# First two hidden units of the second token group in one-pass products, their operands split in the first group's last two units

## The chip, the cores and the metric

The kernel runs on one core of one Trainium2 chip. The metric is the device time of one execution in microseconds, as a median of several runs; less is better. The profile is one execution of its own.

## What is computed

An attention block without softmax, then a feed-forward block over all 4608 tokens:

```python
kv = einsum('bhsd,bhse->bhde', k, v)             # (8, 8, 64, 64)
o = einsum('bhsd,bhde->bhse', q, kv)             # (8, 8, 576, 64)
x = o / sqrt(mean(o * o, axis=-1) + 1e-6) * g_norm
x = x.transpose(0, 2, 1, 3).reshape(4608, 512)
h = x @ w_in                                     # w_in (512, 2048)
g = h * erf(softplus(h))
out = g @ w_out                                  # w_out (2048, 512)
```

q, k, v and g_norm are float32; w_in and w_out come as float64 and are turned into float32 on the chip.

## The kernel before

**Groups and units.** The 4608 tokens are worked off in nine groups of G = 512 (`NG`). Group T below 8 holds the first 512 tokens of batch T; group 8 holds the last 64 tokens of all eight. The 2048 columns of h are FC = 16 tiles of 128. One *unit* is one such tile of one group: h as a 128x512 block, which needs KC = 4 products of 128x128 by 128x512. The first FIRST = 2 groups are run by a loop over n = 0 to 32, with T, f = divmod(n, 16); seven more groups follow in batches of four units.

**Two kinds of product.** In the first group, a unit's h is a plain float32 product (L1031), one accumulation into one PSUM bank, copied out by `nc.scalar.copy`. A *one-pass* product (`hidden`, which calls `product`, L600) works on operands that are split: x into x_high, x_low and x_both, a weight tile into three parts as well. Twelve matmuls go into two banks: n_ps takes 8 (high and low), m_ps takes 4 (both). ACT copies n_ps with a scale, DVE adds m_ps (`add`, L575). The output product of a unit is plain in the first two groups: `project` (L656), four products into four banks that stay open over the units of a group. It runs LAG = 5 units behind h.

**How operands are split.** x: `upper` on ACT (L535), `lower_only` on DVE (L538), `both_only` on DVE (L541). A weight tile: `w_upper` on ACT (L559), `w_lower` with two DVE instructions (L562, L565) and a DMA on SP's queue that stores the parts to DRAM, from where all later groups load them. During the second group all 16 input tiles ("in") and all 16 output tiles ("out") are split, by a list `to_cut[f]` of tiles for each unit. A tile lives in one of four buffers of the pool `w_in_p` (then it is stored by one DMA), or at a place in memory that earlier weight tiles held (`w_place`, three DMAs). Units with f < WHOLE = 2 of the second group, n = 16 and 17, are still plain; from n = 18 on, h is one-pass, with the input tile that was split two units before. Input tiles 0 and 1 are split too, at n = 16 and 17, but only to be stored.

**Memory.** The pool `early` holds the raw weights and the first attention pairs. At n == FC = 16 it is closed, and `late`, `x_new`, `acc`, `w_in_p` and `low` are opened where it was. x of the second group, `xT[1]`, lies in the buffer "b" of the pool `wide`; x_high takes buffer "a", which held `xT[0]`, and x_both takes "b" once the last plain product of the second group has read `xT[1]`.

**Order.** The schedule is manual: each engine runs its instructions in the order in which the program emits them. For unit n: joins of raw weights while they are due (L271 to L282), `w_lower` for up to two weight tiles that `w_upper` took in the unit before, attention pieces, `gates` (L904, h times s of unit n - 4), the product of h, its copy, more splits, softplus (L1065), attention pieces, then `project(n - 5)`. Every fourth unit Erf is run for four units at once (L976), with an ACT table load before and after it. The pieces of attention for the second group's last pair lie around n = 12 to 15: `mean` with Ln, Exp and Square (L476 to L478) at n = 14, and `norm` on DVE (L484, L487, L496), which completes `xT[1]`, at n = 15, with the transpose of the next pair's q (L337). The first pair of the third group is visited at n = 17 (L412 to L426). At n = 16 x_high and x_low are made before h, at n = 17 x_both after it:

```python
if T == FIRST - 1:
    if f == 0:
        x_high = wide.tile([P, KC, G], FP32R, name="x_high", tag="a")
        x_low = low.tile([P, KC, G], FP32R, name="x_low")
        for i in range(0, KC, 2):
            upper(xT[T][:, i : i + 2], x_high[:, i : i + 2])
        for i in range(0, KC, 2):
            lower_only(xT[T][:, i : i + 2], x_high[:, i : i + 2], x_low[:, i : i + 2])
if T == FIRST - 1 and f >= WHOLE:
    n_ps, m_ps = hidden(T, f, turns=False)
```

Of the kernel before, what the change touches and what calls it, by code (L numbers as in the profile page):

```python
# [40 lines left out]
FP32R = mybir.dt.float32r  # L41
# [9 lines left out]
BATCH = 4  # L51
LAG = 5
# [1 line left out]


FIRST = 2
WHOLE = 2
SHIFT = 4096.0
SQ = 32
ORDER = """  # L60
# [9 lines left out]
def kernel(  # L70
# [11 lines left out]
    P = 128  # L82
# [3 lines left out]
    G = J * P  # L86
    R = S - G
    NP = H // 2
    KC = DM // P
    FC = DF // P  # L90
# [9 lines left out]
    wide = ctx.enter_context(tc.tile_pool(name="wide", bufs=1, side="right"))  # L100
# [189 lines left out]
    w_at = {"load": 0, "split": 0, "join": 0}  # L290
# [8 lines left out]
    def weights():  # L299

        w_next("split")
        w_next("join")
        w_next("load")
# [229 lines left out]
    def upper(x, high):  # L533

        nc.scalar.activation(high, x, AF.Copy, scale=1.0 + 2.0**-13)  # L535

    def lower_only(x, high, low):
        nc.vector.tensor_tensor(out=low, in0=x, in1=high.bitcast(FP32), op=ALU.subtract)  # L538

    def both_only(high, low, both):  # L540
        nc.vector.scalar_tensor_tensor(  # L541
            out=both,
            in0=low.bitcast(FP32),
            scalar=SHIFT,
            in1=high.bitcast(FP32),
            op0=ALU.mult,
            op1=ALU.add,
        )
# [80 lines left out]
    def w_lower(which, f):  # L629

        t, x, parts = w_new.pop((which, f))
        lower_w(x, *parts)
        kept = w_kept[which, f] = dram.tile([P, 3, G], FP32, name=f"w_{which}{f}")
        for i in range(3):
            if t is None:
                nc.sync.dma_start(out=kept[:, i], in_=parts[i].bitcast(FP32))
        if t is not None:
            nc.sync.dma_start(out=kept, in_=t.bitcast(FP32))
            if which == "in" and f >= WHOLE:
                w_now[which, f] = [t]  # L640

    def hidden(T, f, turns=True):
# [232 lines left out]

    others = [("in", f) for f in range(WHOLE)]
    others += [("out", f) for f in (*range(FC - BATCH, FC), *range(FC - BATCH))]
    places_w = {3: 0, 5: 1, 6: 0, 8: 1, 9: 2, 10: 0}  # L880
    held_w = {FC - 7: 3, FC - 5: 1}
    to_cut = {f: [] for f in range(FC)}
    for f in range(FC):
        if f < FC - BATCH:
            other = others.pop(0)
            if other[0] == "out" and other[1] in held_w:
                other = (*other, held_w[other[1]])
            to_cut[f] = [other, ("in", f + WHOLE)]
        elif f == FC - BATCH:
            to_cut[f] = [("in", FC - 2), ("in", FC - 1)]  # L890
        if f in places_w:
            to_cut[f].append((*others.pop(0), places_w[f]))
# [22 lines left out]
    def hold_lower(n):  # L915
        lower(hs[n], *g_held[n])
# [60 lines left out]

    for n in range(FIRST * FC + 1):
        T, f = divmod(n, FC)
        if n == FC:  # L980
            early_room.close()
            late = ctx.enter_context(tc.tile_pool(name="late", bufs=1))
            x_new = ctx.enter_context(tc.tile_pool(name="x_new", bufs=1))
            acc = ctx.enter_context(tc.tile_pool(name="acc", bufs=1))
            w_in_p = ctx.enter_context(tc.tile_pool(name="w_in_p", bufs=BATCH))
            low = low_room.enter_context(tc.tile_pool(name="low", bufs=1))
            forms = late.tile([P, 3, KC, G], FP32R, name="x_forms0")
            x_forms[FIRST] = [forms[:, i] for i in range(3)]
        if T < FIRST:
            if f == 0:  # L990
                steps = pieces_of(T + 1)

            if due(0 if n == 2 * (BATCH - 1) else 1):
                weights()
            while kept:
                keep_prepared()
            for piece in steps[f][3]:
                piece()
            for key in list(w_new)[:2]:
                w_lower(*key)  # L1000
            for piece in steps[f][0]:
                piece()
        while due(0):
            weights()
        done = n - LAG + 1
        if T == 0 and done >= 0:
            gates(done)
        if T == FIRST - 1:
            if f == 0:
                x_high = wide.tile([P, KC, G], FP32R, name="x_high", tag="a")  # L1010
                x_low = low.tile([P, KC, G], FP32R, name="x_low")
                for i in range(0, KC, 2):
                    upper(xT[T][:, i : i + 2], x_high[:, i : i + 2])
                for i in range(0, KC, 2):
                    lower_only(xT[T][:, i : i + 2], x_high[:, i : i + 2], x_low[:, i : i + 2])
        if T == FIRST - 1 and f >= WHOLE:
            n_ps, m_ps = hidden(T, f, turns=False)
        elif T < FIRST:

            if n >= AHEAD:  # L1020
                plain[n] = ps_h.tile([P, G], FP32, name="h_ps", tag="h")
                blocks = [(n, c) for c in range(KC)]
            elif n == 0:
                for i, (pool, tag) in enumerate(((ps_now[0], "at"), (ps_now[0], "at"), (ps_o, "o0"))):
                    plain[i] = pool.tile([P, G], FP32, name="h_ps", tag=tag)
                blocks = [(i, c) for c in range(2) for i in range(2)]
                blocks += [(2, 0), (2, 1)] + [(i, 2) for i in range(3)] + [(0, KC - 1)]
            else:
                blocks = [(n, KC - 1)]
            for i, c in blocks:  # L1030
                nc.tensor.matmul(  # L1031
                    plain[i],
                    lhsT=blocks_of(one(w_in_sb, i % FC))[:, c],
                    rhs=xT[T][:, c, :],
                    start=(c == 0),
                    stop=(c == KC - 1),
                )
        if T < FIRST:
            if n == whole:
                old_h = acc.tile([P, BATCH, G], FP32, name="h", tag="e")  # L1040
            h = hs[n] = old_h[:, n - whole] if n >= whole else unit("h_sb")
            s = ss[n] = unit("s_sb")
            if n in plain:
                nc.scalar.copy(h, plain.pop(n))
            else:
                nc.scalar.activation(h, n_ps, AF.Copy, scale=SHIFT - 1.0)
                add(h, m_ps)
            if T == FIRST - 1:
                if f == 1:
                    x_both = wide.tile([P, KC, G], FP32R, name="x_both", tag="b")  # L1050
                    for i in range(0, KC, 2):
                        both_only(x_high[:, i : i + 2], x_low[:, i : i + 2], x_both[:, i : i + 2])
                    x_forms[T] = x_high, x_low, x_both
                if n <= whole + 2:
                    gates(done + max(0, n - whole - 1))
                for key in list(w_new):
                    w_lower(*key)
                for key in to_cut[f]:
                    w_upper(*key)
                if n == whole + 1:  # L1060
                    gates(whole - 2)
            if T == FIRST - 1 and f and f % BATCH == 0:
                erf(range(n - BATCH // 2, n))
                softplus_table()
            nc.scalar.activation(s, h, AF.Softplus)  # L1065
            for piece in steps[f][1]:
                piece()
            for i in range(*{whole + 1: (0, 2), whole + 2: (2, 4)}.get(n, (0,))):
                hold_upper(whole - BATCH + i)
            for i in range(*{whole + 2: (0, 2), whole + 3: (2, 4)}.get(n, (0,))):  # L1070
                hold_lower(whole - BATCH + i)
            if f % BATCH == BATCH - 1 and n < whole:
                apart = T == FIRST - 1 and f < FC - 1
                erf(range(n - BATCH + 1, n + 1 - (BATCH // 2 if apart else 0)))
                if not apart:
                    softplus_table()
            if T == FIRST - 1:
                load_parts("in", {FC - 3: 2, FC - 2: 1, FC - 1: 1}.get(f, 0))
        if LAG <= n < whole - BATCH + LAG:
            T2, f2 = divmod(n - LAG, FC)  # L1080
            last = n - LAG == FC - 1
            project(f2, hs[n - LAG], last)
            if last:
                sums(acc, "e")
                for j in range(J):
                    store(T2, j, es.pop(j))
        if n == FIRST * FC:
            held_sums()
        if T < FIRST:
            for piece in steps[f][2]:  # L1090
                piece()
            fetch_some(4)
# [191 lines left out]
```

## Time and profile before

| what | value |
|---|---|
| median of 3 runs | 904.55 us (904.25 to 904.59) |
| profiled execution, own time | 904.33 us |
| its span | 902.5 us |
| matmuls of plain h (L1031), two groups | 144 records, 592 ns median |
| matmuls of one-pass h and outputs (L600) | 389 to 392 ns mean |
| output products of the first two groups (L656) | 192 records, 595 ns mean |

The span runs from the first to the last instruction; the own time of the profiled execution is 1.83 us longer. A record of a matmul overlaps the next one's, so the step from one start to the next is what a product costs. A plain product of 128x128 by 128x512 is two records, so one plain h is eight. PE is TensorE's matmul side, DVE VectorE, ACT ScalarE, SP the engine whose queue issues nearly all DMAs. In a timeline a line gives the start, the duration, the engine, the line of the kernel and what was done, and in brackets how long the engine stood idle before and what ended that.

### The profile page before, as it was taken

To read this page: it belongs to the slowest core of one execution; us is meant where nothing else is said; L and a number is where in the kernel's file an instruction comes from. 1 tells how busy PE (TensorE), PEld (TensorE's weight loads), DVE (VectorE), ACT (ScalarE), POOL (GpSimd) and SP (SyncE) were. 2 spreads that over 40 slices of the span, in tenths; PEclk is the share of its full clock that TensorE was granted. 3 is DMA by queue.
4 is the path that set the end of the run, shared out by engine and by line. 5 is a ranking of instruction groups with operands and counts; after the bars stand their busy time and mean duration, and the time that the engine had idled before them with its cause. 6 is when DMAs were issued, how large, how long until landed. Compare 5 with 4: busy or idle time off the path is not lost.

```text
span 902.5 us, 13462 instructions
## 1 busy us (share of the span) xinstructions
PE 894.9 (99%) x4954; PEld 671.3 (74%) x4954; DVE 765.2 (85%) x1103; ACT 594.7 (66%) x789; POOL 4.7 (1%) x14
## 2 busy tenths in 40 slices
PE   8999999999999999999999999999999999999998
PEld 4444446566788888888888888888888888888886
DVE  5799958999898888888888888888888888887677
ACT  5976667777766666666766666666666666665552
POOL 2000000000000000000000000000000000000000
PEclk9999999999999999999999999999999999999999
DMA  9967408999699997988899979988897787778871
GB/s 287 300 218 228 108 15 290 366 355 342 240 386 365 335 304 255 382 307 299 279 350 346 319 243 330 372 292 300 284 341 274 270 308 307 288 281 314 326 261 50
DMA packets 137505, 259.89 MB, mean 288 GB/s; under 512 B 78880, under 2 KB 87328, under 8 KB 137440
## 3 DMA queue, kind: packets, MB, share of 16 engines
q1 hardware_dynamic: 136704, 258.09, 81.2%
q8 instruction: 39, 0.64, 0.3%
q10 hardware_dynamic: 544, 0.82, 0.3%
q14 instruction: 26, 0.21, 0.1%
q0 software_dynamic: 192, 0.13, 0.0%
HBM read 224.40 MB, written 34.60 MB: 287 GB/s over the span
## 4 chain that ended last, share of the span: by engine, by line
PE 97%; DVE 1%; ACT 1%; DMA 1%; issue 0%; DVEq 0%; SPq 0%
PE n_ps L600 49%; PE m_ps L600 24%; PE o_ps L656 9%; PE h_ps L1031 6%; PE at_ps L426 2%; PE at_ps L412 2%; PE n_ps L920 1%; PE at_ps L464 1%; PE at_ps L465 1%; PE warm_ps L803 1%; DMA w_raw<-in_moe_w_out_dram 1%; PE o_ps L920 0%; DVE w_e L277 0%; PE o_ps L723 0%; DVE w_in_sb L282 0%; PE ms_ps L730 0%
## 5 line engine op out<-in xcount | busy, mean ns | idle before, releaser
L600 PE MATMUL n_ps<-w_out_parts,g_forms 128*128 128x512 f32 (+1 forms) x936 | 230.7, 389 | 0.0
L600 PE MATMUL n_ps<-x_forms,w_in_parts 128*128 128x512 f32 x896 | 224.0, 392 | 0.0
L600 PEld LDWEIGHTS n_ps<-w_out_parts,g_forms 128*128 128x128 f32 x936 | 173.7, 188 | 35.3
L600 PEld LDWEIGHTS n_ps<-x_forms,w_in_parts 128*128 128x128 f32 x896 | 166.6, 188 | 35.3
L575 DVE TENSOR_TENSOR h<-m_ps,h 128x512 f32<-128x512 f32 x116 | 78.2, 688 | 60.2 <-PE m_ps L600 57.9
L600 PE MATMUL m_ps<-w_out_parts,g_forms 128*128 128x512 f32 x464 | 124.0, 389 | 0.0
L600 PE MATMUL m_ps<-x_forms,w_in_parts 128*128 128x512 f32 x448 | 119.7, 389 | 0.0
L1190 ACT ACTIVATE h<-n_ps 128x512 f32<-128x512 f32 x112 | 66.1, 593 | 75.2 <-PE n_ps L600 75.0
L1195 ACT ACTIVATE s<-h 128x512 f32<-128x512 f32 x112 | 68.3, 629 | 70.0 <-DVE h L575 69.9
L600 PEld LDWEIGHTS m_ps<-w_out_parts,g_forms 128*128 128x128 f32 x464 | 87.1, 188 | 18.5
L600 PEld LDWEIGHTS m_ps<-x_forms,w_in_parts 128*128 128x128 f32 x448 | 84.1, 188 | 17.5
L575 DVE TENSOR_TENSOR e<-m_ps,e 128x512 f32<-128x512 f32 x116 | 80.2, 692 | 15.2 <-PE m_ps L600 5.3
L656 PE MATMUL o_ps<-w_out_sb,h_sb 128*128 128x512 f32 x192 | 86.9, 595 | 0.0
L541 DVE SCALAR_TENSOR_TENSOR g_forms<-g_forms 128x1024 fp32r<-128x1024 f32 x58 | 71.1, 1225 | 2.0
L538 DVE TENSOR_TENSOR g_forms<-h,g_forms 128x1024 fp32r<-128x1024 f32 x58 | 70.6, 1217 | 1.2 <-ACT g_forms L535 1.1
L535 ACT ACTIVATE g_forms<-h 128x1024 fp32r<-128x1024 f32 x58 | 58.4, 1049 | 15.5 <-PE m_ps L600 11.1
L1031 PE MATMUL h_ps<-xT,w_in_sb 128*128 128x512 f32 x144 | 65.1, 596 | 1.2 <-DVE w_in_sb L282 1.1
L570 DVE SCALAR_TENSOR_TENSOR e<-n_ps,e 128x512 f32<-128x512 f32 (+1 forms) x89 | 60.4, 678 | 6.9 <-PE n_ps L600 6.9
L1244 DVE TENSOR_TENSOR h<-h,s 128x1024 f32<-128x1024 f32 x56 | 65.9, 1218 | 0.0
L656 PEld LDWEIGHTS o_ps<-w_out_sb,h_sb 128*128 128x128 f32 x192 | 35.5, 189 | 38.3 <-issue 37.4
L116 ACT ACT_TABLE_LOAD x43 | 55.2, 1283 | 0.8
L1031 PEld LDWEIGHTS h_ps<-xT,w_in_sb 128*128 128x128 f32 x144 | 26.9, 190 | 35.4 <-issue 31.4
(148 smaller groups left out, 1030.7 us busy)
## 6 DMA issues: line engine op xcount, KB each, us to landing
w_out_parts<-w_out SPq DMA_DIRECT2D x116, 768.0 KB, 7.0
w_in_parts<-w_in SPq DMA_DIRECT2D x112, 768.0 KB, 6.6
w_in<-w_new SPq DMA_DIRECT2D x16, 768.0 KB, 4.8
k_sb<-in_k_dram SPq DMA_DIRECT2D x32, 288.0 KB, 5.9
v_sb<-in_v_dram SPq DMA_DIRECT2D x31, 288.0 KB, 6.3
w_raw<-in_moe_w_in_dram SPq DMA_DIRECT2D x16, 512.0 KB, 5.6
w_raw<-in_moe_w_out_dram SPq DMA_DIRECT2D x8, 1024.0 KB, 5.4
out_dram<-e SPq DMA_DIRECT2D x32, 256.0 KB, 3.5
```

The costliest lines, as they stand in the source:

```text
L116: nc.scalar.preload_act_table_set("softplus")
L535: nc.scalar.activation(high, x, AF.Copy, scale=1.0 + 2.0**-13)
L538: nc.vector.tensor_tensor(out=low, in0=x, in1=high.bitcast(FP32), op=ALU.subtract)
L541: nc.vector.scalar_tensor_tensor(out=both, in0=low.bitcast(FP32), scalar=SHIFT, in1=high.bitcast(FP32), op0=ALU.mult, op1=ALU.add,)
L570: nc.vector.scalar_tensor_tensor(out=out_, in0=ps, scalar=scale, in1=out_, op0=ALU.mult, op1=ALU.add)
L575: nc.vector.tensor_tensor(out=out_, in0=ps, in1=out_, op=ALU.add)
L600: nc.tensor.matmul(ps[:, cols], lhsT=weights(form, k), rhs=moving(form, k)[:, cols], start=(form == forms[0] and k == 0), stop=(form == fo ...
L656: nc.tensor.matmul(o_ps[j], lhsT=g[:, j * P : j * P + P], rhs=one(w_out_sb, f), start=(f == 0), stop=last,)
L1031: nc.tensor.matmul(plain[i], lhsT=blocks_of(one(w_in_sb, i % FC))[:, c], rhs=xT[T][:, c, :], start=(c == 0), stop=(c == KC - 1),)
L1190: nc.scalar.activation(h[:, i], n_ps, AF.Copy, scale=SHIFT - 1.0)
L1195: nc.scalar.activation(s[:, i], h[:, i], AF.Softplus)
L1244: nc.vector.tensor_tensor(out=part(h, half), in0=part(h, half), in1=part(s, half), op=ALU.mult)
```

## The change

Units 16 and 17 use `hidden` like the rest of the second group. The input tiles 0 and 1 are put through `w_upper` at n = 14, after softplus, and through `w_lower` at the start of n = 15; the pools are reopened at n = 14 for this, behind a loop that finishes what joins are left. x_high is made at n = 15, after softplus and before the Erf run. At n = 16, x_low and x_both are made, then `project` of unit 11 is issued, then h; the `project` that stood behind h there is left out. The list `others` loses the two input tiles, so the output tiles 12 to 15, 0 and 1 are split up to two units earlier, one a unit; the tiles 14 and 1 go through `w_in_p` instead of a place. From f = 6 on the lists are the same.

```diff
-WHOLE = 2
...
-            if which == "in" and f >= WHOLE:
+            if which == "in":
                 w_now[which, f] = [t]
...
-    others = [("in", f) for f in range(WHOLE)]
-    others += [("out", f) for f in (*range(FC - BATCH, FC), *range(FC - BATCH))]
-    places_w = {3: 0, 5: 1, 6: 0, 8: 1, 9: 2, 10: 0}
+    others = [("out", f) for f in (*range(FC - BATCH, FC), *range(FC - BATCH))]
+    places_w = {6: 0, 8: 1, 9: 2, 10: 0}
...
-            to_cut[f] = [other, ("in", f + WHOLE)]
+            to_cut[f] = [other, ("in", f + 2)]
...
-        if n == FC:
-            early_room.close()
...
         if T == FIRST - 1:
             if f == 0:
-                x_high = wide.tile([P, KC, G], FP32R, name="x_high", tag="a")
                 x_low = low.tile([P, KC, G], FP32R, name="x_low")
                 for i in range(0, KC, 2):
-                    upper(xT[T][:, i : i + 2], x_high[:, i : i + 2])
+                    lower_only(xT[T][:, i : i + 2], x_high[:, i : i + 2], x_low[:, i : i + 2])
+                x_both = wide.tile([P, KC, G], FP32R, name="x_both", tag="b")
                 for i in range(0, KC, 2):
-                    lower_only(xT[T][:, i : i + 2], x_high[:, i : i + 2], x_low[:, i : i + 2])
-        if T == FIRST - 1 and f >= WHOLE:
+                    both_only(x_high[:, i : i + 2], x_low[:, i : i + 2], x_both[:, i : i + 2])
+                x_forms[T] = x_high, x_low, x_both
+                project(f + FC - LAG, hs[n - LAG], False)
             n_ps, m_ps = hidden(T, f, turns=False)
...
-                if f == 1:
-                    x_both = wide.tile([P, KC, G], FP32R, name="x_both", tag="b")
-                    for i in range(0, KC, 2):
-                        both_only(x_high[:, i : i + 2], x_low[:, i : i + 2], x_both[:, i : i + 2])
-                    x_forms[T] = x_high, x_low, x_both
...
             nc.scalar.activation(s, h, AF.Softplus)
+            if n == FC - 2:
+                while w_at["join"] < len(w_order):
+                    weights()
+                early_room.close()
...
+                w_in_p = ctx.enter_context(tc.tile_pool(name="w_in_p", bufs=BATCH))
...
+                for i in range(2):
+                    w_upper("in", i)
...
+            if n == FC - 1:
+                x_high = wide.tile([P, KC, G], FP32R, name="x_high", tag="a")
+                for i in range(0, KC, 2):
+                    upper(xT[1][:, i : i + 2], x_high[:, i : i + 2])
...
-        if LAG <= n < whole - BATCH + LAG:
+        if LAG <= n < whole - BATCH + LAG and n != FC:
```

## The prediction

> **What bounds the kernel now.** I read the busy row first, then the chain that ended last, then the timeline of TensorE around the change, then those of DVE and ACT over the same stretch.
>
> ```profile
> PE 894.9 (99%) x4954; PEld 671.3 (74%) x4954; DVE 765.2 (85%) x1103; ACT 594.7 (66%) x789; POOL 4.7 (1%) x14
> PE 97%; DVE 1%; ACT 1%; DMA 1%; issue 0%; DVEq 0%; SPq 0%
> ```
>
> TensorE is busy 894.9 of 902.5 us and makes up 97% of the chain. So what counts is its own work plus any gap that the change puts into it. The table of stretches says where its 7.6 idle us lie: 3.15 before 50 us, 0.41 from 50 to 110, none from 110 to 218, 0.24 from 218 to 246, none from 246 to 800, 3.81 after 800. The change works at 115 to 160 us, where there is no gap to win: a gain can only be shorter matmul work.
>
> The timeline of TensorE (start, duration, line, count), with the last four plain h and the output products between them:
>
> ```profile
> 118.66 3.60 PE L1031 MATMUL h_ps<-xT,w_in_sb 128*128 128x512 f32 x8
> 122.10 3.60 PE L656 MATMUL o_ps<-w_out_sb,h_sb 128*128 128x512 f32 x8
> 125.53 3.60 PE L1031 MATMUL h_ps<-xT,w_in_sb 128*128 128x512 f32 x8
> 128.96 3.60 PE L656 MATMUL o_ps<-w_out_sb,h_sb 128*128 128x512 f32 x8
> 132.40 3.60 PE L1031 MATMUL h_ps<-xT,w_in_sb 128*128 128x512 f32 x8
> ```
>
> These are unit 15's h, product 10, unit 16's h, product 11 and unit 17's h, 3.43 or 3.44 us from start to start (the shown 3.60 overlaps the next). The chain in order of time has units 19 and 20 in one-pass products:
>
> ```profile
> 147.60 1.84 PE n_ps L600 x8
> 150.37 3.44 PE o_ps L656 x8
> 153.80 1.87 PE n_ps L600 x8
> 156.61 3.43 PE o_ps L656 x8
> ```
>
> From the first n_ps matmul to the next output product is 2.77 and 2.81 us: a one-pass h costs about 2.79 us.
>
> **What the Trainium skill says.** "FP8 and Floating Point Precision", TensorE Precision Notes: a true FP32 product takes four passes of the array, a reduced one truncates its operands. "TensorE: Matmul & The Clock Gate", Back-to-back issue gap: N/2.4 + 2.5 ns, 216 ns for 512 columns, when warm. Four products in four passes are 16 x 0.216 = 3.45 us, and the trace has 3.43; twelve one-pass matmuls would be 2.59 us by the same figure, while the trace has 2.79, which I use. "PSUM — Partial Sum Buffer", PSUM bank collisions: TensorE may not write a bank while another engine reads it, so a product must wait until its two banks are emptied; unit 18 on shows this order. "ScalarE: Activation LUTs", What ACT_TABLE_LOAD costs: an ACTIVATE with immediate scale takes 186 ns + 0.833 ns per column (613 ns at 512), and two in a row overlap by some 93 ns; the trace agrees with 0.62 for one w_new tile and 1.15 for two.
>
> **The change part by part.**
>
> *Removed from TensorE:* two plain h, 2 x 3.43 = 6.86 us. *Added:* two one-pass h. The first follows an output product, as in the fence (2.79). The second follows a one-pass h directly; units 30 and 31 do so, and unit 31 takes 2.78 (220.66 to 223.44). Sum 5.57: **1.29 us less**. The four output products stay; the one for unit 11 goes ahead of unit 16's h and costs the same.
>
> *Are the inputs there in time?* DVE and ACT before (idle time and its cause in brackets):
>
> ```profile
> 115.28 0.69 DVE L904 TENSOR_TENSOR h_sb<-h_sb,s_sb 128x512 f32<-128x512 f32 x1
> 119.58 0.69 DVE L484 SCALAR_TENSOR_TENSOR u<-at_ps,u 128x512 f32<-128x512 f32 x1 [3.61 <-ACT u L478]
> 122.52 0.65 DVE L904 TENSOR_TENSOR h_sb<-h_sb,s_sb 128x512 f32<-128x512 f32 x1
> 129.43 2.36 DVE L538 TENSOR_TENSOR x_low<-xT,x_high 128x1024 fp32r<-128x1024 f32 x2 [6.26 <-ACT x_high L535]
> ```
>
> ```profile
> 115.59 0.63 ACT L1065 ACTIVATE s_sb<-h_sb 128x512 f32<-128x512 f32 x1
> 116.24 1.28 ACT L113 ACT_TABLE_LOAD   x1
> 118.92 0.63 ACT L478 ACTIVATE u<-rms_r 128x512 f32<-128x512 f32 x1
> 122.30 0.58 ACT L1044 COPY h_sb<-h_ps 128x512 f32<-128x512 f32 x1 [1.45 <-PE h_ps L1031]
> 123.56 1.28 ACT L976 ACT_TABLE_LOAD   x1
> 128.34 2.00 ACT L535 ACTIVATE x_high<-xT 128x1024 fp32r<-128x1024 f32 x2
> ```
>
> There are two holes of DVE, 3.61 and 6.26 us, and one of ACT, 1.45. I lay the moved work into them.
>
> - Unit 14, ACT: the two w_upper stand between softplus and the table load, 116.2 to 117.4. Their pool takes over memory of the closed one; the last instruction that reads it is the last join of w_out, 114.14 to 115.36 on DVE, so they don't wait. The loop that finishes the joins finds none left. Ln, Exp and Square of the second group's last pair end 1.15 later, at 120.7 (119.55), the table load at 122.0, still ahead of the copy at 122.30.
> - Unit 15, DVE: two w_lower, 2.66 us (four of 0.69, from 132.31 to 134.97 before), now 116.85 to 119.5, inside the hole of 3.61. Norm then starts at 120.7 instead of 119.58: xT complete at 122.9, the transpose to 123.7, gate of unit 11 done at 124.3 (123.2). Product 11 now starts at 125.53 instead of 128.96: **1.2 us to spare**.
> - Unit 15, ACT: x_high (2.00 us) goes ahead of the Erf table load, 123.55 to 125.55. Erf and the softplus table end at 130.3, where x_high ended before.
> - Unit 16, DVE: x_low 124.6 to 126.9 and x_both to 129.3, twice 2.36. Unit 16's h starts at 128.96 and reads x_both 1.87 later, at 130.8: **1.5 to 2 us to spare**, thanks to product 11 in front of it. Without that product it would start at 125.53 and wait.
> - Unit 17's h starts at 131.75 with no output product before it. Its n_ps bank must have been emptied by ACT, 0.6 us from 130.9 to 131.5; its m_ps bank, needed at 133.6, is emptied by the added DVE sum (0.69) at 132.5. At units 30 and 31 the same order leaves no idle entry on TensorE. I take 0, bounds 0 to 0.2; the gain side is nothing, because back-to-back h is already priced.
> - Added on DVE: two sums of m_ps, 2 x 0.69 = 1.4 us, at 132 and near 136, beside product work. On ACT a scaled copy (0.60) replaces a plain one (0.58).
> - DMA and SP: the two stores of 768 KB move from about 134 and 142 to about 118 and 120. SP issues nothing between 104 and 133.8 and the DMA share from 110 to 125.5 is 0.00, so nothing is queued behind them; POOL has all its 14 instructions before 50 us. What they left, the next k, v and q loads at 135.5, then has the stores of output tile 12 and input tile 2 before it, at about the same time. Output tiles 14 and 1 go through whole tiles, so two stores replace six (4.2 us of SP's issue for three, 0.4 for one). Off the path: bounds -0.2 to +0.2.
> - The buffer of input tile 1 is taken again in unit 17 by input tile 3, which waits for unit 17's last matmul at 134.5; ACT gets there at 134.75. Queued behind it is unit 17's softplus, which waits for DVE until 136.5 anyway.
>
> **Sum.** Against the profiled execution: span 902.5 - 1.29 = 901.2; 1.83 us lie around the span (904.33 - 902.5), so 903.0. The median of the runs is 0.22 above that execution: **903.3 us**, or -0.14%. After 160 us TensorE stands idle only for 0.24 us in 218 to 246 and in the closing stage, so the gain should reach the end. A measurement of this kernel can tell about 0.2%, 1.8 us, from no change.
>
> **The rivals.**
>
> *A. A smaller gain: unit 17 waits for its bank.* If the Erf run slips on ACT, the copy of unit 16 ends later than 131.5, and TensorE waits for it between the two h. For: the copy has 0.25 us, and it stands behind 4.8 us of Erf and tables that end at 130.3. Against: ACT has 0.6 us there, and units 30 and 31 manage. A wait of 0.2 to 1.1 gives 903.5 to 904.4.
>
> *B. Slower: the chain in front of product 11.* The moved w_upper stand ahead of the Ln that norm, the gate of unit 11 and x_high hang on. If the reopened memory makes them wait X, everything moves by X and TensorE stalls by X - 1.2 at product 11. Above X = 2.5 the gain is gone, above 4.3 it is slower by over 0.2%. With one late load of 1024 KB (5.4 us to landing on the page) it is 904.55 - 1.3 + 4.2 = 907.5. Against: the loads that used that memory landed before the joins that read them, and the last join ends at 115.36.
>
> *C. More than the sum.* One-pass h without a change of kind before them run at 2.72 later (245.47 to 248.19); two of those save 1.42, and the 0.24 us wait at 231.8 might go too: 1.66, 902.9. Over 1.81 would need still more that no view shows: a shorter switch between kinds of product at 137 to 141, where one output product took 3.63 instead of 3.43, makes 1.86, 902.7.
>
> *D. The change does less than it says.* If x_low or x_both come after 131, the wait eats the 1.29: about 904.5.
>
> **How the numbers follow.** Main case 0.58 (902.9 to 903.6), A 0.08 and D 0.05, all within 0.2%: same is 0.71. C past 1.81 us: faster is 0.15. B, with any wait of over 3.1 us that I don't see: slower is 0.14. The time is the main case's. The range reaches from a little past C's 902.7, at 902.5, over A and D to 904.9, and leaves out most of B and a little of C.
>
> **What would show it.** Right: 128 matmuls of plain h instead of 144 (8 records for each of 16 units), 24 more of one-pass h; product 11 at about 125.5, no idle entry on TensorE from 110 to 160, and product 12, after the visit of the third group's first pair, 1.3 us earlier than at 137.21. DVE's holes of 3.61 and 6.26 filled. Wrong: an idle entry on TensorE before product 11 (B), between the two h (A) or at the first m_ps (D), each with its releaser; or a later stage whose start moves by another amount than 1.3.

## The result

The changed kernel takes 902.96 us (median of 22 runs, 902.45 to 903.56) against 904.5 us for the kernel before (22 runs): a ratio of 0.9983, with a 95% interval of 0.9977 to 0.9990, or 1.5 us less. The interval alone reaches from 0.9 to 2.1 us, so the traces have to say what the true size is. The profiled execution has a span of 901.3 us instead of 902.5.

The page of the changed kernel, its busy row and its chain (lines after the changed place have moved by a few: L1031 is now L1021, L656 is L655, L600 is L599):

```profile
PE 893.6 (99%) x4962; PEld 672.4 (75%) x4962; DVE 766.7 (85%) x1105; ACT 595.1 (66%) x789; POOL 4.7 (1%) x14
PE 96%; DMA 1%; DVE 1%; ACT 1%; issue 0%; SPq 0%; DVEq 0%
```

TensorE has 1.3 us less to do in eight more instructions (24 one-pass matmuls for 16 records of plain ones), DVE 1.5 us more in two more. The chain in order of time, from unit 15's h to product 12:

```profile
119.08 3.44 PE h_ps L1021 x8
122.52 6.87 PE o_ps L655 x16
129.38 1.84 PE n_ps L599 x8
131.22 0.93 PE m_ps L599 x4
132.15 1.86 PE n_ps L599 x8
134.01 0.93 PE m_ps L599 x4
...
136.23 3.63 PE o_ps L655 x8
```

Products 10 and 11 (the output products of units 10 and 11) run as one piece of 6.87, then come two one-pass h of 2.77 and 2.79, and nothing but TensorE stands in this chain. The dots stand for the small attention products of the third group's first pair. The waits of TensorE from 110 us on have one entry, 0.2 us in the held sums (the output products that the second group's last four units put off to its end), as before.

DVE after (start, duration, what, and in brackets the idle time in front):

```profile
117.03 0.69 DVE L561 SCALAR_TENSOR_TENSOR w_new<-w_new,w_in_sb 128x512 fp32r<-128x512 f32 x1 [0.79 <-ACT w_new L558]
120.87 0.69 DVE L483 SCALAR_TENSOR_TENSOR u<-at_ps,u 128x512 f32<-128x512 f32 x1 [1.09 <-ACT u L477]
123.81 0.65 DVE L902 TENSOR_TENSOR h_sb<-h_sb,s_sb 128x512 f32<-128x512 f32 x1
124.78 2.36 DVE L537 TENSOR_TENSOR x_low<-xT,x_high 128x1024 fp32r<-128x1024 f32 x2 [0.32 <-ACT x_high L534]
127.17 2.36 DVE L540 SCALAR_TENSOR_TENSOR x_both<-x_low,x_high 128x1024 fp32r<-128x1024 f32 x2
```

and ACT after:

```profile
116.38 1.13 ACT L558 ACTIVATE w_new<-w_in_sb 128x512 fp32r<-128x512 f32 x2
122.55 0.59 ACT L1034 COPY h_sb<-h_ps 128x512 f32<-128x512 f32 x1 [0.41 <-PE h_ps L1021]
131.26 0.60 ACT L1036 ACTIVATE h_sb<-n_ps 128x512 f32<-128x512 f32 x1 [0.76 <-PE n_ps L599]
```

The holes of 3.61 and 6.26 us on DVE have become 0.79 + 1.09 and 0.32, that of 1.45 on ACT 0.41. A new one of 2.72 us stands on DVE behind x_both, before the first sum of m_ps at 132.25. x_both is complete at 129.53, and its first reader starts at 131.06.

**A finer measure than the run time.** Single runs of one kernel differ by up to 1 us or more, and part of that arises ahead of the changed part: in this profile unit 15's h already starts 0.26 us later than before, and over all the traces below its start varies by 1.4 us. So I also take the *stretch* from the start of unit 15's h to the first matmul of the held sums (line 920 before, 918 after) out of each trace. On TensorE both points lie outside the changed part, and no kernel here alters what stands beyond them. Each stretch comes from a single trace.

| kernel | unit 15's h | held sums | stretch | against after | median of runs |
|---|---|---|---|---|---|
| before | 118.66 | 223.91 | 105.25 | +1.29 | 904.5 |
| after | 118.92 | 222.88 | 103.96 | 0 | 902.96 |
| e1_moves_only | 119.14 | 224.39 | 105.25 | +1.29 | 904.26 |
| e2_eight_plain | 117.91 | 226.98 | 109.07 | +5.11 | 908.55 |
| e3_product_behind | 118.82 | 224.40 | 105.58 | +1.62 | 904.61 |
| e4_act_late_8 | 119.24 | 229.11 | 109.87 | +5.91 | 908.94 |
| e5_act_late_3 | 119.09 | 223.96 | 104.87 | +0.91 | 904.21 (one run) |
| e6_act_late_6 | 118.56 | 227.01 | 108.45 | +4.49 | 907.20 |
| e7_late_filled | 119.12 | 227.23 | 108.11 | +4.15 | 907.06 |
| e8_copy_late | 119.30 | 223.55 | 104.25 | +0.29 | 903.78 (one run) |

### The profile page after: what moved, and what is told of

The parts are those of the page before. It is cut to its first block, busy times and chain, and to the rows that moved or that the text cites. A ratio compares the mean times of both kernels' runs of the same rounds, so it can differ in the third digit from the quotient of the medians.

```text
span 901.3 us, 13468 instructions
## 1 busy us (share of the span) xinstructions
PE 893.6 (99%) x4962; PEld 672.4 (75%) x4962; DVE 766.7 (85%) x1105; ACT 595.1 (66%) x789; POOL 4.7 (1%) x14
## 3 DMA queue, kind: packets, MB, share of 16 engines
HBM read 224.40 MB, written 34.60 MB: 287 GB/s over the span
## 4 chain that ended last, share of the span: by engine, by line
PE 96%; DMA 1%; DVE 1%; ACT 1%; issue 0%; SPq 0%; DVEq 0%
PE n_ps L599 50%; PE m_ps L599 25%; PE o_ps L655 9%; PE h_ps L1021 5%; PE at_ps L425 2%; PE at_ps L411 2%; PE n_ps L918 1%; PE at_ps L463 1%; PE at_ps L464 1%; DMA q_sb<-in_q_dram 1%; DMA w_raw<-in_moe_w_out_dram 1%; PE o_ps L918 0%; DVE w_e L276 0%; PE o_ps L722 0%; DVE w_in_sb L281 0%; PE ms_ps L729 0%
## 5 line engine op out<-in xcount | busy, mean ns | idle before, releaser
L599 PE MATMUL n_ps<-w_out_parts,g_forms 128*128 128x512 f32 (+1 forms) x936 | 230.7, 389 | 0.0
L599 PE MATMUL n_ps<-x_forms,w_in_parts 128*128 128x512 f32 x896 | 223.9, 392 | 0.0
L599 PEld LDWEIGHTS n_ps<-w_out_parts,g_forms 128*128 128x128 f32 x936 | 173.7, 188 | 35.3
L599 PEld LDWEIGHTS n_ps<-x_forms,w_in_parts 128*128 128x128 f32 x896 | 166.6, 188 | 35.3
L599 PE MATMUL m_ps<-w_out_parts,g_forms 128*128 128x512 f32 x464 | 124.0, 389 | 0.0
L599 PE MATMUL m_ps<-x_forms,w_in_parts 128*128 128x512 f32 x448 | 119.7, 389 | 0.0
L599 PEld LDWEIGHTS m_ps<-w_out_parts,g_forms 128*128 128x128 f32 x464 | 87.1, 188 | 18.5
L599 PEld LDWEIGHTS m_ps<-x_forms,w_in_parts 128*128 128x128 f32 x448 | 84.1, 188 | 17.5
L655 PE MATMUL o_ps<-w_out_sb,h_sb 128*128 128x512 f32 x192 | 86.8, 595 | 0.0
L655 PEld LDWEIGHTS o_ps<-w_out_sb,h_sb 128*128 128x128 f32 x192 | 35.5, 190 | 38.3 <-issue 36.9
L1021 PE MATMUL h_ps<-xT,w_in_sb 128*128 128x512 f32 x128 | 57.9, 596 | 1.1 <-DVE w_in_sb L281 1.1
L1220 ACT ACTIVATE s<-s 128x1024 f32<-128x1024 f32 x50 | 50.6, 1053 | 0.3
```

Of the source, the lines that this page charges most:

```text
L599: nc.tensor.matmul(ps[:, cols], lhsT=weights(form, k), rhs=moving(form, k)[:, cols], start=(form == forms[0] and k == 0), stop=(form == fo ...
L655: nc.tensor.matmul(o_ps[j], lhsT=g[:, j * P : j * P + P], rhs=one(w_out_sb, f), start=(f == 0), stop=last,)
L1021: nc.tensor.matmul(plain[i], lhsT=blocks_of(one(w_in_sb, i % FC))[:, c], rhs=xT[T][:, c, :], start=(c == 0), stop=(c == KC - 1),)
```

## The experiments

My theory: the change pays by the shorter products of two units and by nothing else, and all moved work lies in idle time. The rivals: part of the gain comes from the moves, or the moves cost something that the gain hides; and it was not needed to put product 11 in front of h. The later runs measure how far the cover reaches, because the prediction's main rival, B, rests on it. All diffs are against the changed kernel.

### e1_moves_only: the moves, plain products

```diff
+PLAIN = 2
...
-            if which == "in":
+            if which == "in" and f >= PLAIN:
                 w_now[which, f] = [t]
...
-                x_both = wide.tile([P, KC, G], FP32R, name="x_both", tag="b")
-                for i in range(0, KC, 2):
-                    both_only(x_high[:, i : i + 2], x_low[:, i : i + 2], x_both[:, i : i + 2])
-                x_forms[T] = x_high, x_low, x_both
                 project(f + FC - LAG, hs[n - LAG], False)
+        if T == FIRST - 1 and f >= PLAIN:
             n_ps, m_ps = hidden(T, f, turns=False)
...
+                if f == PLAIN - 1:
+                    x_both = wide.tile([P, KC, G], FP32R, name="x_both", tag="b")
+                    for i in range(0, KC, 2):
+                        both_only(x_high[:, i : i + 2], x_low[:, i : i + 2], x_both[:, i : i + 2])
+                    x_forms[T] = x_high, x_low, x_both
```

> All the moved work of the change (the splits of input tiles 0 and 1 and of x_high in units 14 and 15, the pools reopened at unit 14, product 11 in front of h), but units 16 and 17 stay plain, with x_both after unit 17. Theory (only the shorter products pay, the moved work costs and saves nothing): the time of before, 904.2 to 904.8, and no idle entry on TensorE from 110 to 160 us. Rival (some of the gain comes from the moves themselves, such as fewer DMAs or a relieved DVE): about 903.0, as after. Rival (the moves cost something that the gain hides): over 905.

904.26 us (13 runs), ratio to before 0.9996 (0.9988 to 1.0005), and a stretch of 105.25, the same to the hundredth as before. TensorE has no idle entry there. So the moved splits, the pools reopened early, the other order of products and the changed stores together cost and save nothing in this stretch; the whole 1.29 belongs to the two products. Only x_both is not moved here: it stays behind unit 17, because the plain products still read the buffer that it takes.

### e2_eight_plain: eight plain units instead of none

The same kernel with PLAIN = 8.

> As the changed kernel, but the first eight units of the second group (16 to 23) are plain instead of none, with x_both after unit 23. Theory (each unit that is plain instead of one-pass costs 3.43 - 2.79 = 0.64 to 0.67 us of TensorE and nothing else counts): 903.0 + 8 x 0.65 = 908.2, between 907.8 and 908.6. Rival (the second group is bound by DVE, or the price is that of a wait): clearly less, 904 to 906, or not proportional to the number of units.

908.55 us (5 runs), ratio to before 1.0049 (1.0035 to 1.0063). The stretch is 5.11 longer than after: 0.64 us for each of eight units, as 1.29 / 2 = 0.645 is for each of two. The price is one of TensorE's work and proportional to the number of units. The median is a little above the expected band's middle; this trace has, beyond the stretch, one wait of 0.5 us for a load of w_out_parts that the others don't have.

### e3_product_behind: product 11 behind unit 16's h

```diff
-                project(f + FC - LAG, hs[n - LAG], False)
...
-        if LAG <= n < whole - BATCH + LAG and n != FC:
+        if LAG <= n < whole - BATCH + LAG:
```

> The changed kernel with product 11 behind unit 16's h again, as it was before; all else as after. Theory (product 11 covers the splits of x): h of unit 16 starts at about 126 instead of 129.4 and waits for the second half of x_low (done near 127.2) and for x_both (done near 129.5), so it ends near 130.0 instead of 128.7: 1.3 us of idle TensorE between 125.9 and 130, about 904.3 in all, the gain gone. Rival (there was room enough, the order does not matter): 903.0 and no idle entry.

904.61 us (13 runs), ratio to before 1.0002 (0.9994 to 1.0010): the gain is gone. Unit 16's h now starts at 125.29 and stops twice in its m_ps part, as the timeline of TensorE shows:

```profile
128.35 0.73 PE L599 MATMUL m_ps<-x_both,w_new 128*128 128x512 f32 x2 [0.30 <-DVE x_both L540]
129.49 0.73 PE L599 MATMUL m_ps<-x_both,w_new 128*128 128x512 f32 x2 [0.40 <-DVE x_both L540]
```

The entries name only 0.7 us, since a record overlaps the next, and before them weight loads waited 0.9 us for x_low. From its first n_ps matmul to the next product this h takes 4.77 us (125.29 to 130.06), in the changed kernel 3.17 (128.82 to 131.99): 1.60 of the 1.62 that the stretch lost. The expectation had 1.3. In the changed kernel, the one line that puts the product in front is worth more than the whole gain of the change.

### e4_act_late_8: the chain in front of product 11, 5.3 us late

```diff
                 for i in range(2):
                     w_upper("in", i)
+                for _ in range(8):
+                    upper_w(w_new["in", 1][1], w_new["in", 1][2][0])
```

> The changed kernel with eight more copies of the w_upper of input tile 1 (same input, same output) on ACT at unit 14, in front of the Ln of the last pair: 8 x 0.52 = 4.2 us later there. Theory (the chain Ln, norm, gate, product 11 has 1.5 us to spare): TensorE waits 2.7 us before product 11, with DVE's gate as its releaser, 905.7 to 906.1. Rival (some other chain is tighter, x_high or the Erf run on ACT, and the wait falls elsewhere): idle before unit 16's or 17's h, up to 4.2 us in all, over 906.5. Rival (off the path): 903.0.

908.94 us (5 runs), ratio to before 1.0049 (1.0037 to 1.0062): 3 us above the expectation. Two things were wrong in it. Each copy took 0.66 instead of 0.52, so the table load stood at 123.15 instead of 117.85, 5.30 later; that each copy writes where the one before wrote is the likely reason, but no run tests it apart. And the wait cost more than its length:

```profile
130.13 5.40 PE L655 MATMUL o_ps<-w_out_sb,h_sb 128*128 128x512 f32 x8 [3.86 <-DVE h_sb L902]
```

The releaser is the gate on DVE, as foretold, but the product behind the wait takes 5.40 us where its like takes 3.60. The table of stretches (busy time of PE, PEld, DVE, ACT and POOL, then the granted clock, that is the share of full speed at which TensorE was let run, then the DMA share and GB/s) says why:

```profile
126.00:130.10 4.10, 0.27 (x1) 0.00 (x0) 3.51 (x6) 4.04 (x6) 0.00 (x0) 1.00 0.48 151
130.10:133.00 2.90, 2.87 (x4) 1.33 (x5) 2.87 (x3) 2.87 (x4) 0.00 (x0) 0.54 0.00 0
133.00:134.50 1.50, 1.50 (x3) 0.51 (x3) 1.50 (x2) 1.48 (x4) 0.00 (x0) 0.75 0.00 0
```

With the idle time the granted clock of TensorE falls to half; the fall comes at about 130.35, just after product 11 has begun. From start to start, the wait is 4.03 us (130.13 - 122.67 - 3.43) and the product behind it costs another 1.8 (4.83 to the next h instead of 3.03): 5.83 of the 5.91 that the stretch lost.

### e5_act_late_3 and e6_act_late_6: the same, smaller

The same loop with range(3) and range(6).

> As e4_act_late_8 with three more copies instead of eight. In that run one more copy cost ACT 0.66 us (each writes where the one before wrote) and eight made TensorE idle for 3.86, so 5.30 - 3.86 = 1.44 us were to spare. Theory (a slack of 1.44, then one for one): 3 x 0.66 = 1.99 late, an idle entry of 0.55 us before product 11 with the gate on DVE as releaser, and the product at its usual 3.43. Rival (no slack, or a wait elsewhere): 2 us of idle, or none.

> As e4_act_late_8 with six more copies. 6 x 0.66 = 3.97 late, less 1.44: 2.5 us of idle TensorE before product 11. Theory 1 (the 5.40 instead of 3.43 us of product 11 in e4_act_late_8 came from the idle time before it, and a shorter idle time costs less): product 11 takes under 5.4, and the time is 903.0 + 2.5 + 0 to 1.5 = 905.5 to 907.0. Theory 2 (any idle time of over 2 us sets the clock back in full): 5.4 again, 907.5.

Product 11 in the timelines, first of e5, then of e6:

```profile
126.67 3.70 PE L655 MATMUL o_ps<-w_out_sb,h_sb 128*128 128x512 f32 x8 [0.55 <-DVE h_sb L902]
```

```profile
128.11 5.31 PE L655 MATMUL o_ps<-w_out_sb,h_sb 128*128 128x512 f32 x8 [2.52 <-DVE h_sb L902]
```

The idle entries are 0.55 and 2.52, as expected from 3 and 6 times 0.66. From start to start the waits are 0.71, 2.68 and 4.03 us for 1.99, 3.97 and 5.30 us of delay: the slack is 1.28, 1.29 and 1.27. The clock is the new part (tables of stretches, first e5, then e6):

```profile
126.00:127.00 1.00, 0.45 (x2) 0.30 (x2) 1.00 (x3) 1.00 (x2) 0.00 (x0) 1.00 0.00 0
127.00:128.00 1.00, 1.00 (x3) 0.38 (x2) 1.00 (x2) 0.98 (x2) 0.00 (x0) 1.00 0.00 0
```

```profile
127.50:128.00 0.50, 0.00 (x0) 0.00 (x0) 0.50 (x2) 0.50 (x2) 0.00 (x0) 0.96 0.00 0
128.00:128.50 0.50, 0.39 (x1) 0.39 (x2) 0.50 (x2) 0.50 (x1) 0.00 (x0) 0.50 0.00 0
131.00:131.50 0.50, 0.50 (x2) 0.17 (x1) 0.50 (x1) 0.50 (x2) 0.00 (x0) 0.62 0.00 0
131.50:132.00 0.50, 0.50 (x3) 0.22 (x2) 0.50 (x2) 0.50 (x2) 0.00 (x0) 1.00 0.00 0
```

In e5, of which there is one run, the clock stays at 1.00 behind 0.55 us of idle time. In e6 it falls just before 128.0 and is back at 131.4; in e4 it is low from about 130.35 to 133.75, so some 3.4 us each time. To the next h, product 11 takes 4.74 us in e6 and 4.83 in e4. Behind a wait that leaves the clock at 1.00 it takes 3.14 (e5) and 3.13 (e7 below), 0.1 more than the 3.03 without a wait (130.06 to 133.09 in e3). So the slow clock itself costs 1.6 us in e6 and 1.7 in e4.

e6 takes 907.2 us (5 runs, ratio 1.0030, 1.0018 to 1.0042). That lies between the two theories of its expectation, 907.0 at most and 907.5; product 11, with 5.31 instead of 5.40, is close to the second, the clock set back in full.

### e7_late_filled: the same delay, TensorE kept at work

The loop of e4 with range(8), and in front of product 11:

```diff
+                fill_ps = ps_h.tile([P, G], FP32, name="fill_ps", tag="h")
+                for _ in range(4):
+                    nc.tensor.matmul(
+                        fill_ps, lhsT=one(w_out_sb, 0)[:, 0:P], rhs=one(w_out_sb, 0), start=True, stop=True
+                    )
                 project(f + FC - LAG, hs[n - LAG], False)
```

> As e4_act_late_8, with four plain products of 128x128 by 128x512 on weights, whose result nothing reads, between product 10 and product 11, so that TensorE works for 3.44 of the 3.86 us in which it stood idle. Theory (product 11 took 5.40 us because TensorE had stood idle and its granted clock was 0.50 to 0.75): the granted clock stays at 1.00, product 11 takes 3.43, and the time falls by 2 us to 906.8 to 907.2 although nothing starts earlier. Rival (product 11 was slowed by something else, such as the x splits on DVE and ACT beside it): still 5.4, about 908.9.

907.06 us (8 runs), ratio to before 1.0028 (1.0017 to 1.0038), 1.9 us below e4, although product 11 waits for the same gate and starts as late (timeline, then the table of stretches):

```profile
125.99 3.60 PE L1008 MATMUL fill_ps<-w_out_sb 128*128 128x512 f32 x8
130.02 3.70 PE L655 MATMUL o_ps<-w_out_sb,h_sb 128*128 128x512 f32 x8 [0.43 <-DVE h_sb L902]
```

```profile
130.10:133.00 2.90, 2.90 (x7) 1.35 (x8) 2.87 (x3) 2.87 (x4) 0.00 (x0) 1.00 0.00 0
```

With 3.6 us of work that nothing reads, the clock stays at 1.00 and the record of the product is 3.70 us long. DVE and ACT are as busy beside it as in e4 (2.87 of 2.90 us), so it was the idle time, not the work beside it.

### e8_copy_late: the bank between the two h

```diff
                 if not apart:
                     softplus_table()
+                if n == FC - 1:
+                    for i in range(2):
+                        nc.scalar.activation(forms[:, 0, i], h, AF.Copy, scale=1.0)
```

> The changed kernel with two more copies of a 128x512 block on ACT (to memory that is written again later) behind the softplus table load of unit 15, so before the copy of unit 16's n_ps: 2 x 0.52 to 0.6 us later. ACT had 0.76 idle before that copy in the changed kernel, and the copy ended 0.13 before unit 17's first matmul. Theory (unit 17's h waits for its bank and nothing covers it): an idle entry of 0.2 to 0.5 us on TensorE between the two h, with ACT's copy as releaser. Rival (there is more room than the trace shows): no idle entry.

Unit 17's first matmul comes 1.13 us after unit 16's m_ps begins, instead of 0.93 (131.06 to 131.99 after):

```profile
131.44 1.09 PE L599 MATMUL m_ps<-x_both,w_new 128*128 128x512 f32 x4
132.57 0.50 PE L599 MATMUL n_ps<-x_high,w_new 128*128 128x512 f32 x1
```

ACT's copy of n_ps ends at 132.52, 0.05 before. The expected idle entry does not appear, because the records of the matmuls overlap by more than the wait of 0.2 us. The weight loads of the array, which come ahead of the matmuls, name it: those of n_ps wait 0.5 us for ACT's copy, against 0.2 in the changed kernel. The stretch is 0.29 longer (one run). The copy comes 0.28 later after the start of unit 16's h than in the changed kernel, the matmul 0.20 later, so this place has some 0.1 us to spare there, and a delay of ACT goes through to TensorE from there on.

## Why the prediction was right, step by step

**The bound.** It said that TensorE's own work and new gaps decide. e1 and e2 show it: with the products undone and the moves kept the stretch is that of before, and the price per unit is the same for two and for eight units.

**The sum.** 6.86 - 5.57 = 1.29 us was predicted; the stretch became 1.29 shorter, and the two h take 2.77 and 2.79 in the chain, where 2.79 and 2.78 were put in. Product 12 starts 1.31 us earlier once the 0.26 of the later start is allowed for, as foretold. The 3.45 and 2.59 us that the prediction works out from the skill's issue gap are estimates, and nothing rests on them: the trace has 3.43 and 2.79.

The medians of the runs differ by 1.5, or 0.25 more than the stretch. The interval, 0.9 to 2.1 us, has room for that as scatter, but it is not shown to be scatter. e1, which has the moves without the shorter products, lies 0.11 below before in its own comparison (904.26 against 904.37, interval -1.1 to +0.5), so a small gain of the moves outside the stretch is not excluded; no view shows one. The predicted 903.3 us is 0.34 above the measured time, mostly by this rest.

**The cover.** The laid-out times met the trace within 0.15 us once its start, 0.26 later, is allowed for: w_lower begins at 117.03 (116.85), norm at 120.87 (120.7), gate 11 ends at 124.46 (124.3), x_both at 129.53 (129.3). The slack before product 11, predicted as 1.2 us, is 1.28 by e4 to e6. That x_low and x_both need product 11 in front was said without a price; e3 sets it at 1.62 us.

**The stores.** Priced at nothing; the stretch of e1 agrees, in which they are moved and merged as in the change.

**Rival A**, a wait for unit 17's bank, did not come true, but by little: the prediction gave the copy 0.25 us, the trace has 0.13 between its end and the matmul after it, and e8 shows that some 0.1 of that can be spent. A slip of ACT of a few tenths of a microsecond would have brought it about, so here some luck was needed.

**Rival B** did not come true, since the two w_upper waited for nothing (116.38, right after softplus). Its mechanism and its place are right, its price was too low. The step "TensorE stalls by X - 1.2" leaves out what the stall does to the matmuls behind it. For X = 5.30 it gives 904.55 - 1.3 + 4.1 = 907.4 us; e4 measured 908.94. The missing term is the half clock, 1.7 us, which e7 takes away. So the point from which it is slower by over 0.2% is not X = 4.3; at X = 3.97 (e6) the kernel is already 0.3% slower (0.18% to 0.42%). With X = 1.99 (e5) 0.38 of the 1.29 us are left in the stretch; X = 2.5, where the gain was to be gone, was not tried.

**Rivals C and D.** The other kind of product saves no more than the sum: the second one-pass h takes 2.79, not 2.72, the wait of 0.24 us in the held sums is still there, and product 12 still takes 3.63. Nor did a wait eat the gain (D): x_both was complete 1.5 us before its first reader.

## What to carry to other kernels

Where one engine makes up the whole chain without a gap, price a change by start-to-start times of its instructions, and check the moved work by laying it into the holes of the other engines, instruction by instruction. Before a product whose operands come late, put one whose operands are ready: here one moved line is worth more than the gain it protects. And keep TensorE from standing idle for microseconds: here a stall of 2.5 us cost its own length and then 1.6 us of slow clock behind it.

## What was not expected of the hardware

Around 2.5 and 3.9 us of idle time TensorE ran at half clock for 3.4 us (granted clock 0.50), which cost 1.6 and 1.7 us on top; around 0.55 and 0.43 us (e5, e7) it did not. "TensorE: Matmul & The Clock Gate", What's actually happening, describes such a gate, with half clock after at least one idle window of about 3.4 us in a free-running count, and full clock after some 3.4 us of work.

The length of the slow part agrees, and so does the free-running count. The fall is not tied to the length of the wait: it comes 2.4 us after the last matmul before the wait in e6, still within the wait, and 4.1 us after it in e4, when the next product already runs. The changes of clock that the traces record also lie on one raster: in e4 and e6 the slow part lasts 3.413 us and the full clock before it 122.88 us, 36 times as long; in the eight other traces the full clock lasts 894.29, 897.71 or 901.12 us up to its fall at the end of the program, 262, 263 and 264 times 3.413. There the fall comes 1.8 us after the last matmul in the trace before, 3.4 us after it in e1.

A full idle window, however, was not needed. The 3.413 us that end with the fall held some 2.4 us of idle time in e6, and only 1.8 us of it at the end of the kernel before, whose last matmul ends at 898.70 (table of stretches):

```profile
898.70:900.40 1.70, 0.00 (x0) 0.00 (x0) 0.29 (x1) 0.00 (x0) 0.00 (x0) 1.00 0.53 146
900.50:902.50 2.00, 0.00 (x0) 0.00 (x0) 0.00 (x0) 0.00 (x0) 0.00 (x0) 0.50 0.09 21
```

So by these figures a stall of 1.8 us can be enough, if it lies within one such window. How little is enough, and what becomes of a stall that two windows share, was not measured; no run has one of between 0.55 and 2.5 us in the middle of the work.
